# A filter's transform with tables of its own, taken about time 0, and its rows loaded 112 at a time

## The chip, the cores and the metric

The kernel runs on one core of a Trainium2 chip. The metric is the device time of one execution in microseconds; a time given for a kernel is the median of several runs. Besides it there is one execution taken by the hardware profiler, with every instruction's start and length on each engine: PE (matrix products), DVE (vector), ACT (activations, with tables loaded in sets), POOL (which here mostly issues loads) and SP (which issues stores).

## The reference, cut to what matters

Two layers stand behind each other. The first is an attention without softmax, `out = q (k^T v)`, divided by the root mean square over a head's 64 columns and multiplied by `g_norm`. Its output is `x`, of shape batch 8, sequence 576, width 512. The second layer is

```
proj = x @ w_proj                       # 512 -> 3 * 512
x1, x2, x3 = the three thirds of proj
X2 = rfft(x2, n=576, axis=1)            # along the sequence
H  = rfft(filter_fft, n=576, axis=0)    # of the weights: the same for every batch
x2_conv = irfft(X2 * H, n=576, axis=1)
out = (x1 * x2_conv * x3) @ w_out
```

The change is about `H`: it needs the input `filter_fft` (576 rows of 512 numbers) alone, and is computed once, while batch 0 is on its way.

## The kernel before, in words

Everything is held with at most 128 rows. The sequence of 576 is split by a factor of three: three thirds of 192 (SB), each of them folded about its middle, so that a real transform becomes products with cosines and with sines of half length. Frequencies come in groups g = 0, 1, 2: the multiples of 3 (97 of them, N1), and the others in a group of 128 and one of 64. Times are taken in the middle between samples (the odd numbers of `tvi`), so that time reversal maps the grid onto itself.

The tables are made at the start. `tvi` (L120) holds odd numbers, `kcol` (L155) the frequencies; for three columns c, DVE reduces the angle to one turn (L169 to L172, tile `ang`), and ACT takes the absolute value and two sines (L173, L175, L176) into `IV`, which has 288 columns (TH). `IV` serves the inverse transform, of which it uses 192 columns. For the forward transform `tables()` (L187) turns it around with PE transposes into PSUM tiles `ps_ft`, and DVE copies these into `FW` and `FX` (L205 to L210). Column blocks a = 0, 1, 2 of 128, 128 and 32 times are made; blocks beyond 192 serve the filter only.

The filter: `fa` holds rows of `filter_fft` in the order of the grid and `fc` the rows of reversed time, gathered by an indirect DMA with the row numbers `fidx` (L136 to L148). `fold_filter()` (L315) adds and subtracts them into `ff`. `gen_h(g)` (L332) multiplies `ff` with `FW` into a PSUM tile `ps_h`. As the grid stands half a sample beside time 0, the result has to be turned by a phase: `ph` (L163, L164) holds its cosine and sine, `cf` and `pc` the same times the scale of the inverse transform; ACT takes one product (L355, tile `hu`) and DVE the other with the sum (L356), which gives `HH` and `HM`; ACT makes a negative copy (L358).

What sets the order. Each engine has one queue, and its order is fixed when the program is built, by a scheduler that starts from the program's text and keeps some instructions where they stand (`keep_in_program_order`). PSUM has four slots of two banks (`ps_tile`, and `psp.tile` in `tables`); a tile waits for the reader of the one that had its slot. In batch 0 the text goes: `warm` (products that keep PE busy), `qtr(0)`, `warm`, then for both halves `kv`, `att_o`, `att_r`, `att_x`, `fold`; `tables()`; `proj2(0)` (L363: x2, by PE, copied by ACT); `fold_filter()`; `proj13(0, 0)` and `proj13(0, 1)` (L428 and L434); `gen_h(1)`, `gen_h(0)`, `qtr(1)`, `gen_h(2)`, `kv(1)`; and after it the attention of batch 1 mixed with the transforms `fft(0, g)`, whose products with `HH` and `HM` are L408, L409 and L417. From batch 1 on the filter is only read.

POOL issues all loads. In the order of issue: q of batch 0 in two parts, k and v of batch 0 in six, `w_proj` in three, `fa` in three, `fc` in three, q, k and v of batch 1, `w_out`. There are eight semaphores for such loads, so a load waits until the one issued eight before it has landed. The small integer tables (iota) are made on POOL before the first k load.

Of the kernel before, what the change touches and what calls it, by code (L numbers as in the profile page):

```python
# [15 lines left out]
P = 128  # L16
# [4 lines left out]
def kernel(  # L21
# [95 lines left out]
    tvi = work.tile([P, 2 * SB], I32, name="tvi", tag="yg", bufs=3)  # L117


    nc.gpsimd.iota(tvi, pattern=[[2 * SB, 2], [2, 3], [6, 64]], base=1, channel_multiplier=0)  # L120
# [18 lines left out]
    for a, r0, n, base in ((0, 0, 64, 0), (0, 64, 64, 1), (1, 0, 64, 2), (1, 64, 64, SB), (2, 0, 32, SB + 1)):  # L139
        nc.gpsimd.iota(fidx[r0:r0 + n, a:a + 1], pattern=[[0, 1]], base=S - 1 - base, channel_multiplier=-3)  # L140
    for r0, n, a, na, base, step in ((0, 64, 0, 2, 0, 2), (64, 64, 0, 2, 1, SB - 1), (0, 32, 2, 1, SB + 1, 1)):
        nc.gpsimd.dma_start(out=fa[r0:r0 + n, a:a + na], in_=bass.AP(
            tensor=moe_filter_fft.tensor, offset=moe_filter_fft.offset + base * DM,
            ap=[[3 * DM, n], [step * DM, na], [1, DM]]))
    for a in range(3):
        n = P if a < 2 else 32
        nc.gpsimd.indirect_dma_start(out=fc[:n, a], out_offset=None, in_=moe_filter_fft,
                                     in_offset=bass.IndirectOffsetOnAxis(ap=fidx[:n, a:a + 1], axis=0))  # L148
# [7 lines left out]
    tv = work.tile([P, TH], FP32, name="tv", tag="yg", bufs=3)  # L156
    nc.vector.tensor_copy(out=tv, in_=tvi[:, 0:TH])
    IV = consts.tile([P, 6, TH], BF16)
    asc = consts.tile([P, 3], FP32)
    cf = consts.tile([P, 3, 3], FP32)  # L160
    ph = consts.tile([P, 2, 3], FP32)

    nc.scalar.activation(out=ph[:, 0], in_=kcol, func=AF.Sin, scale=-W0, bias=cosb[:, 0:1])  # L163
    nc.scalar.activation(out=ph[:, 1], in_=kcol, func=AF.Sin, scale=W0)  # L164
    for c, tag in enumerate(("x", "Y", "g13")):

        ang = work.tile([P, 2, TH], FP32, name="ang", tag=tag, bufs=1 if c else 2)
# [9 lines left out]
    tc.keep_in_program_order(nc.scalar.preload_act_table_set("abs_reciprocal_sqrt_and_small"))  # L177
# [6 lines left out]
    FW = consts.tile([P, 3, 6, P], BF16)  # L184
    FX = consts.tile([P, 4, P], BF16)

    def tables():  # L187
        nc.vector.memset(FX[0:96, 0], 0.0)
        fts = [psp.tile([P, 2, 8, P], BF16, name="ps_ft", tag="ps") for _ in range(2)]
        lo, hi = slice(0, 64), slice(64, P)  # L190
        tr = nc.tensor.transpose
        for a in range(3):
            n = P if a < 2 else 32
            ts = slice(a * P, a * P + n)
            d = fts[a // 2][:n, a % 2]
            for i in range(6):
                tr(d[:, i], IV[:, i, ts], ident)
            if a == 0:
                tr(d[96:P, 6], IV[:, 1, 0:32], ident)
                for i in (lo, hi):  # L200
                    tr(d[i, 7], IV[:, 1, 32:96], ident)
            if a == 1:
                for i in (3, 5):
                    tr(d[hi, 6 + i // 5], IV[:, i, P:SB], ident)
            nc.vector.tensor_copy(out=FW[:n, a], in_=d[:, 0:6])  # L205
            if a == 0:
                nc.vector.tensor_copy(out=FX[96:P, 0], in_=d[96:P, 6])
                nc.vector.tensor_copy(out=FX[:, 1], in_=d[:, 7])
            if a == 1:
                nc.vector.tensor_copy(out=FX[hi, 2:4], in_=d[hi, 6:8])  # L210
# [104 lines left out]
    def fold_filter():  # L315
        ff = hst['ff'] = work.tile([P, 2, 3, DM], BF16, name="ff", tag="ff")
        for i, op in enumerate((nc.vector.tensor_add, nc.vector.tensor_sub)):
            for r, c in ((slice(0, P), slice(0, 2)), (slice(0, 32), slice(2, 3))):
                tc.keep_in_program_order(op(out=ff[r, i, c], in0=fa[r, c], in1=fc[r, c]))

        nc.vector.memset(asc, 2.0 / S)
        nc.vector.memset(asc[0:1, 0:1], 1.0 / S)
        nc.vector.memset(asc[96:97, 0:1], 1.0 / S)
        for i in range(2):
            nc.vector.tensor_mul(out=cf[:, i], in0=ph[:, i], in1=asc)
        nc.vector.tensor_scalar_mul(out=cf[:, 2], in0=cf[:, 1], scalar1=-1.0)
        pc = hst['pc'] = consts.tile([P, 4], FP32, name="pc")
        for r, o in ((slice(0, 64), (0, 1, 2, 0)), (slice(64, P), (2, 0, 0, 1))):
            for i in range(4):
                nc.gpsimd.tensor_copy(out=pc[r, i:i + 1], in_=cf[r, o[i], 2:3])  # L330

    def gen_h(g):  # L332

# [3 lines left out]
        for ri in range(2):  # L337
            for a in range(3):
                m = P if a < 2 else 32
                kw = dict(start=(a == 0), stop=(a == 2))  # L340
                if g < 2:
                    nc.tensor.matmul(hp[:n, ri], FW[:m, a, 2 * g + ri, 0:n], ff[:m, ri, a], **kw)
                else:
                    for dup in range(2):
                        nc.tensor.matmul(hp[dup * NM:(dup + 1) * NM, ri], FW[:m, a, 4 + ri, ri * NM:(ri + 1) * NM], ff[:m, ri, a], **kw)
# [298 lines left out]
```

## Time and profile before

| | |
|---|---|
| median of 9 runs | 241.28 us (239.31 to 243.04) |
| the profiled execution | 241.06 us |
| its span | 239.0 us |
| busy: PE, DVE, ACT, POOL | 216.4, 197.1, 156.3, 74.1 us |
| TensorE clock granted, mean | 0.976 |
| moved by loads and stores | 27.17 MB |

The stages, from the busy time of each engine in five stretches of the span (us; the last columns are the share of time in which the DMA engines were busy, which can pass 1 since packets overlap, and GB/s):

| stretch | what runs | PE | DVE | ACT | POOL | DMA | GB/s |
|---|---|---|---|---|---|---|---|
| 0 to 21 | tables, attention of batch 0 | 15.6 | 14.8 | 12.2 | 15.6 | 1.15 | 151 |
| 21 to 33.5 | x2 of batch 0, first projections | 10.1 | 9.0 | 3.7 | 9.2 | 1.36 | 221 |
| 33.5 to 43.3 | the filter, q and kv of batch 1 | 7.3 | 4.5 | 6.8 | 5.2 | 1.48 | 196 |
| 43.3 to 59.4 | transforms of batch 0, attention of batch 1 | 13.5 | 15.1 | 9.9 | 8.1 | 1.38 | 161 |
| 59.4 to 239 | batches 1 to 7 | 170.0 | 153.7 | 123.7 | 36.0 | 0.54 | 93 |

A row of the timeline gives the start and the length in microseconds, the engine, the line of the kernel, the operation, the tile written and the tiles read, how many instructions are merged in the row, and in brackets how long the engine stood idle before it and what it waited for. A row of the chain of waits gives start and length of a step in the chain that ended last; "issue" is time in which the engine waited for nothing that the profile shows. A row of the waits gives who waited for whom, the total, how often, and the longest. In the table of stretches an engine's busy time is followed by the number of its instructions, then come the granted clock, the DMA share and GB/s.

### The profile page before, as it was taken

What the parts mean: (1) busy time and instruction counts of PE and PEld (TensorE: products, weight loads), DVE (VectorE), ACT (ScalarE), POOL (GpSimd) and SP (SyncE); (2) the same over time, 40 slices, a digit from 0 to 9 for tenths busy, and PEclk for the clock granted to TensorE, in tenths of its full rate; (3) what the DMA queues carried; (4) which work ended last, traced back from release to release, by engine and by line L of the source; (5) the groups of instructions that cost most, each with busy time, mean ns of one, the idle gap of its engine ahead of it and who ended that gap; (6) DMA issues with size and microseconds to landing.
All of it is one profiled execution on the core that took longest, in us unless ns stands there. A gap on an engine that the chain in (4) does not pass through costs nothing.

```text
span 239.0 us, 4900 instructions
## 1 busy us (share of the span) xinstructions
PE 216.4 (91%) x1960; PEld 129.5 (54%) x1960; DVE 197.1 (82%) x376; ACT 156.3 (65%) x237; POOL 74.1 (31%) x96
## 2 busy tenths in 40 slices
PE   4978788796999999999999999999999999999960
PEld 1434354364566756665667566656675666566420
DVE  6759474699989798979797989797979897999860
ACT  2754528881797779786977697769776977642520
POOL 7963892491190019000910091001200120021010
PEclk9999999797999999999999999999999999999996
DMA  6999999999099139915993399350033003400345
GB/s 65 161 197 237 215 192 197 191 182 109 3 143 189 55 88 141 196 51 134 109 182 96 91 110 175 103 134 0 4 88 88 3 0 91 132 0 3 95 122 178
DMA packets 45559, 27.17 MB, mean 114 GB/s; under 512 B 22274, under 2 KB 40706, under 8 KB 45538
## 3 DMA queue, kind: packets, MB, share of 16 engines
q0 software_dynamic: 40256, 17.70, 58.7%
q1 hardware_dynamic: 5122, 8.92, 13.9%
q8 instruction: 15, 0.25, 0.4%
q10 hardware_dynamic: 160, 0.26, 0.4%
q14 instruction: 6, 0.05, 0.1%
HBM read 33.69 MB, written 9.44 MB: 180 GB/s over the span
## 4 chain that ended last, share of the span: by engine, by line
PE 63%; ACT 16%; DMA 8%; DVE 5%; POOL 3%; issue 2%; POOLq 0%; DVEq 0%
PE ps_x L428 20%; PE ps_out L488 10%; ACT qT L256 6%; PE ps_x L378 5%; DMA fc<-in_moe_filter_fft_dram,fidx 5%; DMA km<-in_k_dram 3%; PE ps_o L265 3%; PE ps_x L369 3%; PE ps_x L384 2%; ACT kvblk L234 2%; PE ps_r L280 2%; ACT osb L271 2%; PE ps_invo L454 2%; PE ps_inve L454 2%; PE ps_x L372 2%
## 5 line engine op out<-in xcount | busy, mean ns | idle before, releaser
L428 PE MATMUL ps_x<-x,wp 128*128 128x288 bf16 x512 | 68.0, 286 | 2.0 <-DVE FX L210 2.0
L428 PEld LDWEIGHTS <-wp 128*128 128x128 bf16 x512 | 49.8, 98 | 15.8 <-issue 3.1
L411 POOL TENSOR_TENSOR Y<-tpw 128x1024 bf16<-128x1024 f32 (+1 forms) x9 | 21.2, 2357 | 68.9 <-PE ps_x L428 43.2
L434 DVE TENSOR_TENSOR g<-ps_x,x 128x576 bf16<-128x576 f32 x32 | 24.2, 755 | 9.9 <-ACT x L432 9.8
L70 POOL DMA_DIRECT2D km<-in_k_dram x9 | 7.8, 871 | 64.7 <-PE ps_kv L223 64.2
L432 ACT CAST x<-ps_x 128x576 bf16<-128x576 f32 x32 | 20.7, 647 | 10.9 <-PE ps_x L428 10.9
L488 PE MATMUL ps_out<-wo,yg 128*128 128x512 bf16 x112 | 26.6, 379 | 0.0
L281 ACT ACTIVATE rstd<-ps_r,bias_eps 128x576 bf16<-128x576 f32 x32 | 23.3, 742 | 4.8 <-PE ps_r L280 4.7
L496 ACT COPY ot<-ps_out 128x1024 f32<-128x1024 f32 (+1 forms) x17 | 15.9, 937 | 13.8 <-PE ps_out L488 13.8
L266 ACT ACTIVATE sq<-ps_o 128x576 bf16<-128x576 f32 x32 | 20.7, 653 | 6.0 <-PE ps_o L265 5.9
L408 DVE TENSOR_TENSOR tpw<-ps_X,HH 128x1024 f32<-128x1024 f32 (+1 forms) x16 | 19.6, 1223 | 5.3 <-PE ps_X L406 4.4
L271 ACT ACTIVATE osb<-ps_o,g_col 128x576 bf16<-128x576 f32 x28 | 20.8, 742 | 0.0
L409 DVE TENSOR_TENSOR tpw<-ps_X,HH 128x1024 f32<-128x1024 f32 (+1 forms) x16 | 19.4, 1215 | 0.0
L458 ACT COPY os<-ps_invo 128x576 f32<-128x576 f32 x14 | 9.0, 641 | 12.7 <-PE ps_x L372 5.1
L265 PE MATMUL ps_o<-qT,kvblk 128*128 128x288 bf16 x64 | 13.2, 293 | 3.7 <-ACT kvblk L234 2.0
L488 PEld LDWEIGHTS <-yg 128*128 128x128 bf16 x112 | 10.8, 98 | 10.4
L378 PE MATMUL ps_x<-wp,ab 128*128 128x512 bf16 x64 | 15.5, 381 | 0.5 <-DVE ab L307 0.4
L256 ACT COPY qT<-ps_qT 128x1152 bf16<-128x1152 bf16 x14 | 15.1, 1122 | 0.1
L535 PE MATMUL ps_w<-kvblk,ind 128*128 128x512 bf16 x33 | 11.0, 484 | 3.7 <-DVE ind L103 3.4
L79 POOL DMA_DIRECT2D qb<-in_q_dram x16 | 12.6, 788 | 5.0 <-DMA wp<-in_moe_w_proj_dram 3.0
L280 PE MATMUL ps_r<-sq,ind 128*128 128x288 bf16 x64 | 13.3, 290 | 0.9 <-ACT osb L271 0.5
L374 ACT CAST x<-ps_x 128x1024 bf16<-128x1024 f32 x8 | 8.1, 1016 | 9.0 <-PE ps_x L372 9.0
(177 smaller groups left out, 421.0 us busy)
## 6 DMA issues: line engine op xcount, KB each, us to landing
out_dram<-ot SPq DMA_DIRECT2D x28, 256.0 KB, 3.2
qb<-in_q_dram POOLq DMA_DIRECT2D x16, 288.0 KB, 7.3
km<-in_k_dram POOLq DMA_DIRECT2D x7, 512.0 KB, 6.2
vm<-in_v_dram POOLq DMA_DIRECT2D x7, 512.0 KB, 8.6
wp<-in_moe_w_proj_dram POOLq DMA_DIRECT2D x3, 512.0 KB, 11.4
out_dram<-ot SPq DMA_DIRECT2D x10, 128.0 KB, 2.9
km<-in_k_dram POOLq DMA_DIRECT2D x2, 256.0 KB, 5.9
kt<-in_k_dram POOLq DMA_DIRECT2D x8, 64.0 KB, 5.7
```

The costliest lines, as they stand in the source:

```text
L256: nc.scalar.copy(out=o_, in_=i_)
L265: nc.tensor.matmul(op[:, h, 0:TH], kvblk[b % 2][:, j], s['qT'][:, 2 * (j % 2) + j // 2, h * TH:(h + 1) * TH], start=True, stop=True)
L266: nc.scalar.activation(out=s['sq'][:, j].rearrange("p (a b) -> p a b", a=2), in_=op[:, :, 0:TH], func=AF.Square)
L271: nc.scalar.activation(out=o_, in_=op[:, :, 0:TH], func=AF.Copy, scale=g_col)
L281: nc.scalar.activation(out=s['rstd'][:, j].rearrange("p (a b) -> p a b", a=2), in_=r2[:, :, 0:TH], func=AF.Abs_reciprocal_sqrt, scale=1.0 ...
L378: nc.tensor.matmul(pp[:, h], ab[:, j, h * SB:h * SB + P], wp[:, j, DM:2 * DM], start=(j == 0), stop=(j == NDC - 1))
L408: nc.vector.tensor_mul(out=t_[:n, 0], in0=xp[:n], in1=HH[:n, g, 1:3])
L411: nc.gpsimd.tensor_add(out=Y[:n, 2 * g:2 * g + 2], in0=t_[:n, :, 0], in1=t_[:n, :, 1])
L428: nc.tensor.matmul(pp[:, h, 0:TH], w_, x[:, j, h * TH:(h + 1) * TH], start=(j == 0), stop=(j == NDC - 1))
L432: nc.scalar.copy(out=x1, in_=pp[:, :, 0:TH])
L434: nc.vector.tensor_mul(out=st[b]['g13'][:, dc].rearrange("p (a b) -> p a b", a=2), in0=pp[:, :, 0:TH], in1=x1)
L488: nc.tensor.matmul(pp[:, cc], yg[:, dc, c * P:(c + 1) * P], wo[:, dc], start=(dc == 0), stop=(dc == NDC - 1))
```

## The change

The filter's rows are taken about time 0: row n is folded with row 576 - n instead of 575 - n. The phase falls away, and with it `ph`, `cf`, `pc`, `hu` and the pairs of ACT and DVE operations that applied it. Its transform gets tables of its own, `FH`, for 97 times by three and all 289 frequencies: DVE makes the angles in `filter_angles()`, called behind `qtr(0)`, and ACT the sines in `filter_tables()`, called in front of `tables()`. ACT's set of functions has been changed by then, so `filter_tables()` loads the set for sines again, and after it the other one. Since rows 0 and 288 are their own partners, two rows of the cosines are halved.

`IV` has 192 columns now and `FW` two column blocks instead of three. `fa` is loaded in one DMA, 112 rows of three sequence rows each (1536 numbers), `fc` in three gathers of 112 rows; 97 of the 112 are used. In the last part of batch 0 `gen_h(2)` goes in front of `qtr(1)`.

```diff
-    tvi = work.tile([P, 2 * SB], I32, name="tvi", tag="yg", bufs=3)
-    nc.gpsimd.iota(tvi, pattern=[[2 * SB, 2], [2, 3], [6, 64]], base=1, channel_multiplier=0)
+    tvi = work.tile([P, SB], I32, name="tvi", tag="yg", bufs=3)
+    nc.gpsimd.iota(tvi, pattern=[[2, 3], [6, 64]], base=1, channel_multiplier=0)
+    NF = N1 + SB
+    kri = work.tile([P, NF], I32, name="kri", tag="yg", bufs=3)
+    nc.gpsimd.iota(kri[:, 0:N1], pattern=[[3, N1]], base=0, channel_multiplier=0)
+    nc.gpsimd.iota(kri[:, N1:NF], pattern=[[1, 2], [3, SB // 2]], base=1, channel_multiplier=0)
+    tci = consts.tile([P, 3], I32)
+    nc.gpsimd.iota(tci, pattern=[[1, 3]], base=0, channel_multiplier=3)
...
-    for a, r0, n, base in ((0, 0, 64, 0), (0, 64, 64, 1), (1, 0, 64, 2), (1, 64, 64, SB), (2, 0, 32, SB + 1)):
-        nc.gpsimd.iota(fidx[r0:r0 + n, a:a + 1], pattern=[[0, 1]], base=S - 1 - base, channel_multiplier=-3)
-    for r0, n, a, na, base, step in ((0, 64, 0, 2, 0, 2), (64, 64, 0, 2, 1, SB - 1), (0, 32, 2, 1, SB + 1, 1)):
-        nc.gpsimd.dma_start(out=fa[r0:r0 + n, a:a + na], in_=bass.AP(
-            tensor=moe_filter_fft.tensor, offset=moe_filter_fft.offset + base * DM,
-            ap=[[3 * DM, n], [step * DM, na], [1, DM]]))
+    nc.gpsimd.iota(fidx, pattern=[[-1, 3]], base=S, channel_multiplier=-3)
+    nc.gpsimd.memset(fidx[0:1, 0:1], 0)
+    NL = 112
+    nc.gpsimd.dma_start(out=fa[:NL], in_=bass.AP(
+        tensor=moe_filter_fft.tensor, offset=moe_filter_fft.offset, ap=[[3 * DM, NL], [1, 3 * DM]]))
     for a in range(3):
-        n = P if a < 2 else 32
-        nc.gpsimd.indirect_dma_start(out=fc[:n, a], out_offset=None, in_=moe_filter_fft,
-                                     in_offset=bass.IndirectOffsetOnAxis(ap=fidx[:n, a:a + 1], axis=0))
+        nc.gpsimd.indirect_dma_start(out=fc[:NL, a], out_offset=None, in_=moe_filter_fft,
+                                     in_offset=bass.IndirectOffsetOnAxis(ap=fidx[:NL, a:a + 1], axis=0))
...
-    IV = consts.tile([P, 6, TH], BF16)
+    IV = consts.tile([P, 6, SB], BF16)
...
-        ang = work.tile([P, 2, TH], FP32, name="ang", tag=tag, bufs=1 if c else 2)
+        ang = work.tile([P, 2, SB], FP32, name="ang", tag=tag, bufs=1 if c else 2)
...
+    def filter_angles():
+        nc.vector.tensor_copy(out=kr, in_=kri)
+        nc.vector.tensor_copy(out=tcol, in_=tci)
+        a_, r_ = (work.tile([P, 3, NF], FP32, name="fang", tag="ot", bufs=3)[:N1] for _ in range(2))
+        for a in range(3):
+            nc.vector.tensor_scalar_mul(out=a_[:, a], in0=kr[:N1], scalar1=tcol[:N1, a:a + 1])
+        nc.vector.tensor_scalar(out=r_, in0=a_, scalar1=1.0 / S, scalar2=MAGIC, op0=ALU.mult, op1=ALU.add)
+        nc.vector.tensor_scalar(out=r_, in0=r_, scalar1=MAGIC, scalar2=-1.0 * S, op0=ALU.subtract, op1=ALU.mult)
+        nc.vector.tensor_tensor(out=r_, in0=r_, in1=a_, op=ALU.add)
+        fang['ar'] = a_, r_
+
+    def filter_tables():
+        a_, r_ = fang['ar']
+        tc.keep_in_program_order(nc.scalar.preload_act_table_set("trig_and_small"))
+        keep = tc.keep_in_program_order
+        keep(nc.scalar.activation(out=a_, in_=r_, func=AF.Abs))
+        keep(nc.scalar.activation(out=FH[:N1, :, 1], in_=r_, func=AF.Sin, scale=2 * W0))
+        keep(nc.scalar.activation(out=FH[:N1, :, 0], in_=a_, func=AF.Sin, scale=-2 * W0, bias=cosb[:N1, 0:1]))
+        rsqrt_set()
+        for p in (0, 96):
+            nc.vector.tensor_scalar_mul(out=FH[p:p + 1, 0, 0], in0=FH[p:p + 1, 0, 0], scalar1=0.5)
...
     def tables():
...
+        for i in range(2, 6):
+            tr(d0[:, i], IV[:, i, 0:P], ident)
+        tr(d0[0:96, 0], IV[:, 0, 0:96], ident)
+        tr(d0[96:P, 6], IV[:, 1, 0:32], ident)
+        for r in (lo, hi):
+            tr(d0[r, 7], IV[:, 1, 32:96], ident)
+        for i in range(2, 6):
+            tr(d1[lo, i], IV[:, i, P:SB], ident)
+        for i in (3, 5):
+            tr(d1[hi, 6 + i // 5], IV[:, i, P:SB], ident)
+        cp(out=FW[:, 0, 2:6], in_=d0[:, 2:6])
+        cp(out=FW[lo, 1, 2:6], in_=d1[lo, 2:6])
+        cp(out=FX[hi, 2:4], in_=d1[hi, 6:8])
+        cp(out=FW[0:96, 0, 0], in_=d0[0:96, 0])
+        cp(out=FX[96:P, 0], in_=d0[96:P, 6])
+        cp(out=FX[:, 1], in_=d0[:, 7])
...
     def fold_filter():
         ff = hst['ff'] = work.tile([P, 2, 3, DM], BF16, name="ff", tag="ff")
         for i, op in enumerate((nc.vector.tensor_add, nc.vector.tensor_sub)):
-            for r, c in ((slice(0, P), slice(0, 2)), (slice(0, 32), slice(2, 3))):
-                tc.keep_in_program_order(op(out=ff[r, i, c], in0=fa[r, c], in1=fc[r, c]))
...
+            tc.keep_in_program_order(op(out=ff[:N1, i], in0=fa[:N1], in1=fc[:N1]))
...
     def gen_h(g):
...
-                    nc.tensor.matmul(hp[:n, ri], FW[:m, a, 2 * g + ri, 0:n], ff[:m, ri, a], **kw)
+                    nc.tensor.matmul(hp[:n, i], FH[:m, a, 1 - i, f0:f0 + n], ff[:m, 1 - i, a], **kw)
...
-            nc.scalar.activation(out=u[:n, i], in_=hp[:n, ri], func=AF.Copy, scale=c1)
-            nc.vector.scalar_tensor_tensor(out=o_, in0=hp[:n, 1 - ri], scalar=c2, in1=u[:n, i], op0=ALU.mult, op1=ALU.add)
-        if g < 2:
-            nc.scalar.activation(out=HH[:n, g, 2], in_=HH[:n, g, 0], func=AF.Copy, scale=-1.0)
+        if g == 2:
+            nc.scalar.activation(out=HM, in_=hp, func=AF.Copy, scale=2.0 / S)
+            return
+        nc.scalar.activation(out=HH[:n, g, 0:2], in_=hp[:n], func=AF.Copy, scale=asc[:n] if g == 0 else 2.0 / S)
+        nc.vector.tensor_scalar_mul(out=HH[:n, g, 2], in0=HH[:n, g, 0], scalar1=-1.0)
...
     qtr(0)
+    filter_angles()
     warm(9)
...
+    filter_tables()
     tables()
...
             gen_h(0)
+            gen_h(2)
             qtr(1)
-            gen_h(2)
             kv(1)
```

## The prediction

> **What bounds the kernel now.** The profiled execution took 241.06 us, its span 239.0: 2.06 us lie around the span and are left alone. The rows of 40 slices show PE at nine tenths from slice 10 on, so everything after about 60 us is PE's and identical in both programs (the built order on each engine differs only in the names of DMA semaphores there). What the change touches ends before 45 us, so I read that stretch of the chain of waits:
>
> ```profile
> 7.84 7.20 DMA km<-in_k_dram
> ...
> 17.28 11.08 DMA fc<-in_moe_filter_fft_dram,fidx
> ...
> 28.48 0.13 DVE ff L319
> 28.61 1.02 issue
> 29.62 0.55 DVE FW L205
> 30.17 0.01 issue
> 30.19 0.30 DVE FX L210
> 30.49 0.04 issue
> 30.53 3.10 PE ps_x L428 x24
> 33.63 3.43 PE ps_h L342 x12
> ...
> 43.25 0.53 PE ps_o L265 x2
> ```
>
> The reader is to see one thread: the gathered filter rows fc land at 28.36; only then DVE can run ff; queued behind that first ff on DVE stand the copies of FW and FX, which hold a PSUM slot that L428 needs. PE stands still from 28.53 to 30.53. The groups of waits confirm both ends:
>
> ```profile
> DVE ff L319 <- DMA fc<-in_moe_filter_fft_dram,fidx: 3.3, 1, 3.3
> ...
> PE ps_x L428 <- DVE FX L210: 2.0, 1, 2.0
> ```
>
> From 43.25 (the first ps_o of batch 1) DVE runs almost without a gap until batch 1's projection starts at 59.40; its first product, at 45.22, waits for ps_X behind ps_o. So **the change is worth what it moves ps_o at 43.25.**
>
> **The change, part by part.**
>
> *Startup.* IV, ang and tv shrink from 288 to 192 columns. With a tensor-tensor at 448 ns for 288 and 1226 for 1024, DVE costs 0.144 us plus 1.057 ns a column; the angle operations lose about 1 us, and casts and two of the three new L196 products take it up again (0.31 + 0.17 + 0.8). Worth nothing either way: PE warms up until 9.4 and qT is copied at 10.15. POOL's iotas gain 0.5 us net (0.51 for 384 columns, 0.12 for one, so 0.31 + 0.22 + 0.31 + 0.12 and gaps against 0.51), before the first k load. The last first-half load (vt, issued at 7.16, 5.0 us to land) is there at 12.16, wanted at 12.74: hidden by 0.08; without that cover at most 0.5.
>
> *filter_angles on DVE.* In the built order an L197 and an L198 (97x867) stand before and between the two copies of kvblk at 13.14, an L199 behind. No row has 867 columns. L170 takes 295 ns for 288: 0.89 if all of it scales, 0.6 if 0.144 is fixed; the row's fixed part is the better founded, I take 0.6. L197 fits before 13.14, L198 delays the second copy and with it ps_o and all of batch 0's attention by **0.6** (0.3 at the least, 1.0 at the most). L199 (0.144 + 867 x 1.057 = 1.06) hides while ACT squares.
>
> *tables().* 14 transposes before the first projection instead of 15, none in the middle of it instead of 8 (saves PE 0.6). But two FW copies now stand ahead of the second x and d_ on DVE, and the first waits for PE's transposes, which end near 22.05. Copy 0.4, x 0.7, copy 0.4: d_ starts at 23.55 instead of 22.25. Everything behind it (ab, rr) is **1.3** later, the 0.6 included. From PE's rows: L378 at 24.7, rr's L369 at 25.6, then L372 0.6, L378 0.5, L384 1.0, four groups of L428 of 1.03: PE reaches the filter at **32.3** (before: 33.47). FX and FW wait for the cosine instead of fc, and are done near 27.0; the stall of 2.0 is gone.
>
> *filter_tables on ACT.* Two table loads, Abs and two Sin of 867 columns come between the last rstd (20.65, now 21.25) and the first copy of x2. ACT at 0.43 for 288 and 0.65 for 576 gives 0.2 + 0.78 ns a column; starts 0.1 apart inside: 0.78 + 0.78 + 0.97 (0.09 more for a bias column, as L281 against L266).
>
> ```profile
> 10.32 0.61 ACT L176 ACTIVATE IV<-ang,cosb 128x288 bf16<-128x288 f32 x1
> 10.95 1.28 ACT L177 ACT_TABLE_LOAD   x1
> 14.24 1.19 ACT L266 ACTIVATE sq<-ps_o 128x576 bf16<-128x576 f32 x2 [2.01 <-PE ps_o L265]
> ```
>
> The row: a load costs 1.28 and starts 0.02 after the activation in front of it. So 1.28 + 2.53 + 1.28 = 5.09, done at 26.34; x2 is ready at 26.7. It fits in ACT's idle 5.31 us. The rule that speaks against this edit is in the Trainium skill, "ScalarE: Activation LUTs", What ACT_TABLE_LOAD costs: a switch of sets is 1.28 us plus a drain of 1.38, about 2.66, so functions should be batched by set. The trace shows no drain ahead of the load, and none can be seen behind it, since ACT then idles until 14.24. By the rule ACT ends at 29.1, x2's three copies at 31.7 instead of 28.8, three groups of L428 wait a little each, and PE is at the filter by 33.2: 0.4 past the landing path below. I take the row; the rule costs 0.4 of the gain.
>
> *The loads.* fa and fc grow from 576 KB each to 672 (112 rows of 6 KB; three gathers of 112 rows), in fewer DMAs. POOL lets a load go when the one eight before it has landed; there are two fewer, so the gathers go out near 13 to 17 instead of 15.9 to 20. That gains nothing by itself: wp's last part lands at 24.15 (10.85 + 13.3), and fa and fc behind it in the same queue took 4.4 us for 1152 KB (to 28.55). 1344 KB take 5.1: **29.3**. Bounds: 28.4 if 6 KB rows move faster and the deeper queue fills the DMA share that sinks to 1.0 around 25, 31 if they move at the 196 GB/s of the loads before. The next q, k and v go out earlier, behind them; kv(1) needs v by 38, landed at 37.6 before.
>
> *ff.* Two operations of 97x1536, 1.69 apart, 1.77 the last (0.144 + 1536 x 1.057): done 3.5 after landing, **32.8**. Before, four operations and two copies took until 32.93. So the filter starts at 32.8, by landing, with PE ready 0.5 sooner.
>
> *gen_h and behind it.* Gone: six L355, six L356, POOL's eight pc copies (3.26 us, hidden). New: three ACT copies of 1024 columns and two small DVE products, hidden. gen_h(2) goes ahead of qtr(1), so on ACT the copy HM stands ahead of qT. From the start of the filter: 3.43 (L342) + 1.75 (L345's 1.84 less its overlap) + 1.05 for HM (L374: 1.02) + 2.1 (qT twice) + 0.75 (kvblk) + 0.05 = 9.15; before it was 43.25 - 33.47 = 9.78. With L378's 0.237 us a matmul in place of L342's 0.286 it is 8.5. ps_o at 42.0 or 41.3; the middle, **1.6 us earlier**.
>
> **Sum.** 241.06 - 1.6 = 239.5. The median of the runs shown, 241.28, lies 0.2 above this execution: forecast 239.7. Ends: startup 0.3 to 1.0 and table drains touch only PE's side, which has 0.5 to spare; landing 28.4 to 31 moves the sum by +0.5 (then PE binds) to -1.7.
>
> **Rivals.**
>
> 1. *The gain is larger because PE's clock holds.* After the idle stretch before 43.25 PE runs at half speed:
>
> ```profile
> 42.00:43.00 1.00, 0.00 (x0) 0.00 (x0) 0.31 (x1) 0.99 (x4) 0.85 (x1) 1.00 1.50 196
> 43.00:44.00 1.00, 0.75 (x3) 0.37 (x4) 0.45 (x1) 0.66 (x2) 1.00 (x3) 0.71 1.63 185
> 44.00:45.00 1.00, 1.00 (x4) 0.11 (x2) 0.67 (x1) 1.00 (x3) 0.59 (x1) 0.50 1.71 186
> 45.00:46.00 1.00, 1.00 (x6) 0.62 (x5) 0.86 (x2) 0.59 (x2) 0.00 (x0) 0.50 1.65 189
> ```
>
> (The third number from the end is the granted clock.) With no hole between gen_h and qtr the drop may not come: ps_o to ps_X then takes about 1.2 instead of 1.9, total gain 2.4: 238.9. Against: 1.7 us of idle before ps_o remain.
>
> 2. *The gain is eaten up by the same clock at another place.* PE now waits for ab from about 23.0 to 24.7. A drop there for 3 us (as long as the one above) costs 1.5 us: PE at the filter by 33.8, gain 0.6: 240.7. For: two such gaps (42.0 and 54.3) were followed by half clock. Against: the gap of 2.0 at 28.53 was not.
>
> 3. *Slower: the landing.* One mechanism: the 112-row transfers move no faster than the loads in front. 1344 KB at 196 GB/s from 24.15 plus the 0.5 us that POOL starts late is 31.5, and with an engine trailing by another 0.5, 32.0. Every microsecond past 28.8 counts in full; ps_o is late from 30.9 on. 32.0 gives 35.5 for ff, 44.6 for ps_o, 1.35 late: 242.6. For: the profile has no 6 KB row, and DMA never rests up to there. Against: the 2 KB rows of the same tensor moved at 238 to 291 GB/s between 21 and 26.
>
> **How the numbers follow.** Forecast (gain 0.9 to 2.2) 0.50, rival 1 0.13, rival 2 0.22, rival 3 0.10, something unlisted 0.05. What a measurement can tell from no change is 0.5%, 1.2 us. Faster by more: most of the forecast and rival 1, 0.58; within: the rest of it and rival 2, 0.30; slower: 0.12. The range 238.4 to 241.6 leaves out rival 3 and the ends of rival 1.
>
> **What would show it.** PE without a stall of 2 us on FX; kvblk's second copy about 0.6 us late; ACT's block of two loads some 5.1 us long and no wait of PE on x2; DVE ff waiting for fc until about 29.3; gen_h starting within 0.1 of ff's end; batch 1's first ps_o near 41.7; an equal distance from there to the end. Wrong, if L428's matmuls or x2's copies end after ff, or fc lands outside 28.4 to 31.

## The result, and the profile after

The changed kernel takes 238.53 us (median of 17 runs, 237.44 to 242.01); the kernel before, run beside it, 240.81 (54 runs). The ratio is 0.9899, with an interval of 0.9874 to 0.9924: 2.4 us (1.8 to 3.0) or 1.0% faster. The forecast was 239.7, a gain of 1.6 us on the 241.28 known then: the direction was right and the median lies just inside the lower end of the range (238.4), but the size was too small. The profiled execution took 238.56 us, its span 236.6 (before: 239.0), mean clock 0.977.

The same stretch of the chain of waits, now of the changed kernel (start, length, what):

```profile
16.46 13.34 DMA fc<-in_moe_filter_fft_dram,fidx
...
29.92 1.26 DVE ff L350
31.18 0.41 issue
31.60 1.76 DVE ff L350
33.36 0.04 issue
33.41 2.78 PE ps_h L364 x12
36.19 1.44 PE ps_h L368 x12
37.63 0.02 issue
37.65 1.02 ACT HM L370
38.68 2.03 ACT qT L288 x2
40.71 0.25 ACT kvblk L266
...
41.39 0.65 PE ps_o L297 x2
```

The chain runs through the very steps of the forecast: fc's landing, ff, the filter's matmuls, HM, qT, kvblk, ps_o. But look at the starts. The kernel before had, on PE's timeline:

```profile
33.47 3.58 PE L342 MATMUL ps_h<-ff,FW 128*128 128x512 bf16 x12
```

The filter begins at 33.41, where it began at 33.47: nearly nothing was gained up to there. From there to ps_o it takes 7.98 us instead of 9.78. So ps_o is 1.86 us earlier, but with other parts than forecast: the forecast had 0.67 at the filter's start, where 0.06 came, and 0.95 behind it, where 1.80 came. The waits of the changed kernel for 22 to 46 us:

```profile
DVE ff L350 <- DMA fc<-in_moe_filter_fft_dram,fidx: 2.2, 1, 2.2
...
PE ps_o L297 <- ACT kvblk L266: 2.0, 1, 2.0
```

The stall on FX is gone. PE still stands for 2.0 us ahead of ps_o, for ScalarE. Behind ps_o the distance is kept: VectorE's d_ starts 1.76 earlier (49.56), its u 1.78 (57.48), kv of batch 2 2.00 (61.68). In the one profiled execution of before, PE ran at half clock from 57 to 60.8, and not in that of after; the step from 1.78 to 2.00 goes with it. From there to PE's last matmul it is 168.2 us in both traces, as in those of all runs here (168.17 to 168.23): what happens behind kv of batch 2 is only shifted. The remaining 0.4 of the span lies behind PE's end, at the last stores: 7.10 us before, 6.73 after, and 6.68 to 7.06 in the other runs. So the last 0.6 of the 2.4 us differ from execution to execution, and the runs do not show that they are the change's.

Why was the filter not sooner? At the start, filter_angles() delays kvblk's second copy, as said: batch 0's first ps_o comes at 14.28 instead of 13.79 (0.49; 0.6 was predicted). Then this happens (PE's timeline and stretches of the changed kernel; in the stretches the third number from the end is the granted clock):

```profile
14.28 1.14 PE L297 MATMUL ps_o<-qT,kvblk 128*128 128x288 bf16 x4 [1.22 <-DVE kvblk L264]
...
28.99 4.09 PE L443 MATMUL ps_x<-x,wp 128*128 128x288 bf16 x32
...
14.00:15.00 1.00, 0.72 (x4) 0.46 (x5) 0.97 (x2) 0.03 (x1) 0.70 (x2) 0.57 1.34 183
15.00:16.00 1.00, 1.00 (x4) 0.43 (x3) 0.66 (x2) 1.00 (x2) 1.00 (x1) 0.50 1.24 201
16.00:17.00 1.00, 1.00 (x5) 0.58 (x4) 1.00 (x2) 0.38 (x2) 0.69 (x2) 0.50 1.23 205
17.00:18.00 1.00, 1.00 (x4) 0.30 (x2) 0.20 (x1) 1.00 (x2) 1.00 (x2) 0.72 1.26 208
```

PE has stood for 1.2 us and runs on at half clock, where before it had 1.00 throughout. d_ starts at 24.37 instead of 22.25: 2.1 late, where 1.3 was predicted, and PE is ready for the filter at 33.08 instead of 32.3. Meanwhile fc lands at 29.80 (29.3 predicted), and ff ends at 33.36 (32.8). The two paths end 0.3 us apart.

The half clock is not the program's alone. Nine kernels, the changed one and eight below, have this startup as it is here, and in the profiles of all of them PE stands for 1.22 or 1.23 us ahead of this ps_o. In six of them half clock followed, and L443 was done 18.8 to 18.9 us after ps_o's start. In three the clock stayed at 1.00, and it took 17.8 to 18.0, so that PE was ready at 31.9 to 32.4. One of the three (PE's timeline of the run below that puts the order of ff's halves on top of the loads held back):

```profile
14.29 0.66 PE L299 MATMUL ps_o<-qT,kvblk 128*128 128x288 bf16 x4 [1.22 <-DVE kvblk L266]
...
28.00 4.09 PE L445 MATMUL ps_x<-x,wp 128*128 128x288 bf16 x32
```

The block of two table loads on ScalarE (timeline of the changed kernel):

```profile
22.16 1.28 ACT L204 ACT_TABLE_LOAD   x1
23.45 0.93 ACT L206 ACTIVATE fang<-fang 97x867 f32<-97x867 f32 x1
...
25.10 1.01 ACT L208 ACTIVATE FH<-fang,cosb 97x867 bf16<-97x867 f32 x1
26.13 1.28 ACT L182 ACT_TABLE_LOAD   x1
27.58 1.01 ACT L389 CAST x<-ps_x 128x1024 bf16<-128x1024 f32 x1 [0.16 <-PE ps_x L387]
```

5.25 us from the first load to the end of the second; 5.09 were predicted by the row, 7.85 by an estimate from the Trainium skill's rule of a drain at each switch ("ScalarE: Activation LUTs", What ACT_TABLE_LOAD costs). No drain is seen ahead of a load (0.02 us), and none behind: the next operation starts 0.01 us after the first load, and the copy behind the second waits 0.16 for PE. The row was right to take.

### The profile page after: what moved, and what is told of

Its sections match the earlier page's. It is cut to its first block, busy times and chain, and to the rows that moved or that the text cites. A ratio compares the mean times of both kernels' runs of the same rounds, so it can differ in the third digit from the quotient of the medians.

```text
span 236.6 us, 4864 instructions
## 1 busy us (share of the span) xinstructions
PE 213.6 (90%) x1951; PEld 129.3 (55%) x1951; DVE 195.7 (83%) x377; ACT 158.9 (67%) x235; POOL 70.6 (30%) x86
## 3 DMA queue, kind: packets, MB, share of 16 engines
q1 hardware_dynamic: 5122, 8.92, 14.3%
## 4 chain that ended last, share of the span: by engine, by line
PE 62%; ACT 15%; DVE 7%; POOL 6%; DMA 6%; issue 2%; POOLq 0%; DVEq 0%
PE ps_x L443 19%; PE ps_out L503 10%; ACT qT L288 6%; DMA fc<-in_moe_filter_fft_dram,fidx 6%; PE ps_x L393 6%; PE ps_o L297 3%; PE ps_x L399 2%; PE ps_x L384 2%; ACT kvblk L266 2%; PE ps_r L312 2%; ACT osb L303 2%; PE ps_invo L469 2%; PE ps_inve L469 2%; ACT sq L298 2%; PE ps_kv L255 2%
## 5 line engine op out<-in xcount | busy, mean ns | idle before, releaser
L443 PE MATMUL ps_x<-x,wp 128*128 128x288 bf16 x512 | 67.8, 286 | 0.0
L443 PEld LDWEIGHTS <-wp 128*128 128x128 bf16 x512 | 49.8, 98 | 13.6 <-issue 0.9
L297 PE MATMUL ps_o<-qT,kvblk 128*128 128x288 bf16 x64 | 13.8, 305 | 4.8 <-ACT kvblk L266 2.7
L321 DVE TENSOR_TENSOR x<-osb,rstd 128x1152 bf16<-128x1152 bf16 x16 | 12.3, 767 | 1.0 <-ACT rstd L313 1.0
```

The lines of the kernel that those rows point to most:

```text
L297: nc.tensor.matmul(op[:, h, 0:TH], kvblk[b % 2][:, j], s['qT'][:, 2 * (j % 2) + j // 2, h * TH:(h + 1) * TH], start=True, stop=True)
L443: nc.tensor.matmul(pp[:, h, 0:TH], w_, x[:, j, h * TH:(h + 1) * TH], start=(j == 0), stop=(j == NDC - 1))
```

## The experiments

Theory A: the filter starts when ff and PE are both there, and from its start to ps_o ScalarE's copies and PE's matmuls make the chain. The rivals differ from run to run and stand in the expectations. All ratios are against the kernel before, run beside each.

**The order of work.** In the changed kernel:

```diff
             gen_h(0)
-            gen_h(2)
             qtr(1)
+            gen_h(2)
```

> The changed kernel with gen_h(2) put behind qtr(1) again. Theory A (behind the filter's start ScalarE's copies are a chain, and the change took copies out of it; their order matters little): the same five copies of ScalarE stand in another order and the 0.31 us in which ScalarE waited for ps_h of L368 goes; batch 1's first ps_o stays at 41.0 to 41.4 us, ratio to the kernel before 0.988 to 0.990. Theory B (the new order is a good part of the gain): ps_o 0.7 us or more later than in the changed kernel, ratio 0.992 or more.

The filter started at 33.59 and ps_o came at 41.14, as A had it: 7.55 us instead of 7.98, so the new order costs 0.4 here. But the ratio was 0.9961 (0.9941 to 0.9981), 1.5 us worse than the changed kernel. Something behind ps_o took back more than was gained; it is found below. Its rows:

```profile
33.59 2.78 PE L364 MATMUL ps_h<-ff,FH 97*128 97x512 bf16 x12
...
41.14 0.42 PE L297 MATMUL ps_o<-qT,kvblk 128*128 128x288 bf16 x2 [1.55 <-ACT kvblk L266]
...
46.89 4.35 DVE L321 TENSOR_TENSOR x<-osb,rstd 128x1152 bf16<-128x1152 bf16 x1
```

The same move alone in the kernel before:

```diff
             gen_h(0)
-            qtr(1)
             gen_h(2)
+            qtr(1)
```

> The kernel before with nothing but the new order, gen_h(2) ahead of qtr(1). Theory A (ScalarE's conversions are the chain): L345 still waits about 1.1 us or more for the PSUM tile that VectorE's L356 lets go, and qT now stands behind two more L355 of 0.7; ps_o 1 to 2 us later than 43.25, ratio 1.004 to 1.008. Theory B (the order is a good part of the gain): ps_o 0.7 us or more earlier, ratio 0.997 or less.

Measured: 1.0076 (1.0047 to 1.0104), 1.8 us slower. ps_o came at 45.76, later than theory A had it: 1.26 of the 2.51 us are the new order's (11.04 from the filter's start instead of 9.78), and the filter started 1.25 late because in this execution PE ran at half clock from 30.4 to 33.5. The order is no part of the gain.

**The stall on FX, alone.** In the kernel before, `keep_in_program_order` around the copies of FW and FX:

> The kernel before with the copies of FW and FX held in program order, so that they stand ahead of ff on VectorE: the stall of 2.0 us at L428 alone is taken away. Theory A: PE is ready for the filter near 31.6, ff ends near 31.9, gen_h starts near 31.9 instead of 33.47, everything behind it is as far away as before; ratio 0.993 to 0.995 (1.2 to 1.6 us). Theory B (the stall's gain is taken back behind it, by the loads of k and v or by ScalarE): ratio 0.998 to 1.000.

Measured: 0.9939 (0.9918 to 0.9959), 1.5 us. Its trace (PE's timeline):

```profile
31.02 3.70 PE L343 MATMUL ps_h<-ff,FW 128*128 128x512 bf16 x12
36.94 1.84 PE L346 MATMUL ps_h<-ff,FW 128*64 128x512 bf16 x12 [1.09 <-DVE HH L357]
40.91 0.42 PE L266 MATMUL ps_o<-qT,kvblk 128*128 128x288 bf16 x2 [1.38 <-ACT kvblk L235]
```

The filter starts at 31.02, even sooner than the 31.9 expected, since the first products need only the first half of ff; ps_o is 2.34 earlier than in before. So the stall was worth all that was hoped from it. (In the two profiled executions the distance is kept: kv of batch 2 comes 2.33 earlier. That the ratio gives 1.5 is a matter of executions: the profiled one of before lies 0.6 above its median here, this one 0.4 below.) The changed kernel removes it too, and pays it back: its PE is ready only at 33.08, its larger load of fc lands 1.4 us later than before (29.80 against 28.36), and its gen_h takes first the half of ff that is made last (`1 - i` in L364), so that no product can start on the first half made.

**The startup.** In the changed kernel `filter_angles()` moved behind the first half of batch 0:

```diff
     qtr(0)
-    filter_angles()
     warm(9)
...
         fold(0, jj)
+        if jj == 0:
+            filter_angles()
```

> The changed kernel with filter_angles() behind the first half of batch 0, so that its L198 does not stand between the copies of kvblk. Theory A (the filter's start is held by fc's landing at 29.8 plus 3.5, with PE ready only 0.3 sooner): the half clock from 14 to 17.5 goes, PE is ready 0.5 to 1.5 sooner, and gen_h still starts at 33.3 to 33.5; ratio 0.988 to 0.992, as the changed kernel. Theory F (the startup's delay is paid in full at the end): ratio 0.985 or less.

The clock stayed at 1.00 from 14 to 18, and PE was ready at 32.0, 1.1 sooner. It waited for ff:

```profile
34.29 1.91 PE L364 MATMUL ps_h<-ff,FH 97*128 97x512 bf16 x8 [2.29 <-DVE ff L350]
```

In this execution fc landed near 30.7, so the filter began later still, at 34.29, outside the expected stretch, and ps_o came at 42.27. The ratio was 0.9900 (0.9858 to 0.9942), the changed kernel's. The startup's delay is hidden behind the landing. (Though its ps_o is 0.88 later, VectorE's first product behind it, tpw, starts at 43.49, as in the changed kernel's profile, 43.48, where PE ran at half clock between the two.) With the loads of fa and fc moved ahead as well (`load_wp` is the loop that is taken out, for the thirds named):

```diff
-    for part in (1, 0, 2):
-        load_w(wp[:, :, part * DM:(part + 1) * DM], ...)
+    load_wp(1)
     (loads of fa and fc)
+    load_wp(0, 2)
```

> The changed kernel with its two startup prices taken away: filter_angles() stands behind the first half of batch 0, so that it does not come between the two copies of kvblk, and fa and fc are loaded ahead of the first and last third of w_proj. Theory A (the filter starts when both ff and PE are there; fc's landing at 29.8 and PE at 33.1 each hold it near 33.4): kvblk's second copy by 13.95, no half clock from 14 to 17.5, fc lands by 26, gen_h starts at 31.5 to 32.2 and the first ps_o stands at 39.5 to 40.2 instead of 41.39. The total then depends on whether GpSimd's additions meet VectorE's x: without it 0.983 to 0.985, with it up to 0.996. Theory B (PE is late for w_proj instead): gen_h at 33.0 or later.

ff now started at 27.32 and waited for no landing. But then w_proj's last third was late:

```profile
PEld L447 <- DMA wp<-in_moe_w_proj_dram: 1.0, 1, 1.0
```

gen_h began at 33.2 to 33.4 and ps_o stood at 41.18: theory B. All these loads are issued by GpSimd into one queue, and here what was moved forward pushed another wait into its place. The ratio was 0.9935 (0.9901 to 0.9969), with x of L325 (L321 elsewhere) stretched to 4.48 us.

**The order of ff's halves.** In the changed kernel:

```diff
-        for i, op in enumerate((nc.vector.tensor_add, nc.vector.tensor_sub)):
+        for i, op in ((1, nc.vector.tensor_sub), (0, nc.vector.tensor_add)):
```

> The changed kernel with the difference of ff made ahead of the sum, since its gen_h takes the difference first. Theory A (ff and PE both hold the start): the first six products of gen_h need only the first operation, done 1.8 after fc's landing, so the start is PE's, 33.0 to 33.5, whatever the landing; where PE is ready before ff's second half the second six still wait for it. Gain 0.1 us where ff and PE end together as in the profile of the changed kernel, 0.5 to 1.0 in executions whose fc lands after 30.3: ratio 0.986 to 0.990. Rival: an earlier ps_o meets the lock-out of VectorE's x and the ratio is 0.993 or more.

VectorE's ff started at 30.33, late, and the filter all the same at 32.96:

```profile
32.96 2.98 PE L364 MATMUL ps_h<-ff,FH 97*128 97x512 bf16 x12
...
41.15 0.42 PE L297 MATMUL ps_o<-qT,kvblk 128*128 128x288 bf16 x2 [1.34 <-ACT kvblk L266]
```

The start is PE's now, and the order of the halves was why the landing bound it. The ratio, 0.9887 (0.9828 to 0.9946), is not told apart from the changed kernel's. The rival's mechanism was there in this profile, x of L321 lasting 4.07 us; what it cost the interval doesn't tell.

**The pace of the matmuls.** In the changed kernel's gen_h, leaving out the third chunk's rows from 32 on:

```diff
-                m = N1 if a == 0 else N1 - 1
+                m = (N1, N1 - 1, 32)[a]
```

> The changed kernel with 32 rows instead of 96 in the third chunk of gen_h's sums; rows 32 on of that chunk are left out of the filter. It asks why a matmul of gen_h took 0.286 us before (rows 128, 128, 32) and 0.232 after (97, 96, 96). If a chunk of 32 rows breaks the pace: L364 x12 back at 3.3 to 3.5 us. If the pace came from the tables' layout or the transfers: 2.7 to 2.9 us.

```profile
34.10 3.60 PE ps_h L364 x12
37.70 1.79 PE ps_h L368 x12
...
43.26 0.42 PE ps_o L297 x2
```

With fewer rows to multiply, the twelve matmuls take 3.60 us instead of 2.78, at a granted clock of 1.00 in both. A chunk of 32 rows between chunks of 96 breaks the pace (0.300 us each instead of 0.232). And the whole stage, 34.10 to 43.26, is 9.16 us, where the forecast had 9.15. That the two agree to 0.01 is chance: the two groups of matmuls took 0.2 more than the forecast's terms, what follows them 0.2 less. It is one execution.

**ScalarE's conversion.** In the kernel before, plain copies out of ps_h, leaving out the turn by the phase (shown in extracts):

```diff
-            nc.scalar.activation(out=u[:n, i], in_=hp[:n, ri], func=AF.Copy, scale=c1)
-            nc.vector.scalar_tensor_tensor(out=o_, in0=hp[:n, 1 - ri], scalar=c2, in1=u[:n, i], ...)
...
-            nc.scalar.activation(out=HH[:n, g, 2], in_=HH[:n, g, 0], func=AF.Copy, scale=-1.0)
...
+        nc.scalar.activation(out=HH[:n, g, 0:2], in_=hp[:n], func=AF.Copy, ...)
+        nc.vector.tensor_scalar_mul(out=HH[:n, g, 2], in0=HH[:n, g, 0], scalar1=-1.0)
```

> The kernel before with plain copies out of ps_h in place of the phase: three copies on ScalarE as in the changed kernel, and the negative on VectorE, instead of six L355, six L356 and two L358; tables, loads, order and rows are those of before. The turn by the phase is left out of the filter. Theory A (ScalarE's conversion is what stands between the filter's start and ps_o): the start stays at 33.5, ps_o comes at 41.7 to 42.0 instead of 43.25, all behind it as much earlier; ratio 0.993 to 0.996. Theory E (what counted was the pace of the matmuls and the tables): ps_o at 43.0 or later, ratio 0.998 or more.

```profile
33.73 3.58 PE L342 MATMUL ps_h<-ff,FW 128*128 128x512 bf16 x11
...
42.08 0.42 PE L265 MATMUL ps_o<-qT,kvblk 128*128 128x288 bf16 x2 [1.25 <-ACT kvblk L234]
```

From the filter's start to ps_o it took 8.35 us instead of 9.78: the conversion is worth 1.4 there. Yet the ratio was 0.9993 (0.9952 to 1.0033), neither theory's at the end. The profiled execution was the shortest of its twelve (239.59 against a median of 241.29), and even in it d_ took 3.15 us.

**What takes a gain at ps_o back.** In the changed kernel the copies of qT of batch 1 went to VectorE (`if b == 0` became `if b < 2` in qtr):

> The changed kernel with the two copies of qT of batch 1 on VectorE instead of ScalarE. Theory A (ScalarE's chain HM, qT, kvblk sets ps_o): kvblk starts when kv(1) ends near 39.3, ps_o at 39.9 to 40.1 instead of 41.39, and all behind it as much earlier; ratio 0.983 to 0.985. Theory B (PE, or the landing of k and v, would end as late anyway, or the half clock takes it back): ps_o later than 40.8, ratio 0.988 or more.

ps_o came at 39.96, as A had it. And the ratio was 0.9961 (0.9942 to 0.9980), worse than the changed kernel. VectorE's and GpSimd's timelines in this run:

```profile
45.71 5.31 DVE L321 TENSOR_TENSOR x<-osb,rstd 128x1152 bf16<-128x1152 bf16 x1
...
45.03 2.36 POOL L426 TENSOR_TENSOR Y<-tpw 128x1024 bf16<-128x1024 f32 x1
...
48.05 2.35 POOL L426 TENSOR_TENSOR Y<-tpw 97x1024 bf16<-97x1024 f32 x1
```

and in the changed kernel itself:

```profile
48.02 0.95 DVE L321 TENSOR_TENSOR x<-osb,rstd 128x1152 bf16<-128x1152 bf16 x1
48.89 0.74 DVE L449 TENSOR_TENSOR g<-ps_x,x 128x576 bf16<-128x576 f32 x1
49.56 2.25 DVE L331 TENSOR_TENSOR d__656<-x 128x768 bf16<-128x768 bf16 x1
...
45.99 2.37 POOL L426 TENSOR_TENSOR Y<-tpw 128x1024 bf16<-128x1024 f32 x1 [1.02 <-ACT rstd L313]
...
49.02 2.36 POOL L426 TENSOR_TENSOR Y<-tpw 97x1024 bf16<-97x1024 f32 x1
```

and d_ in the kernel before:

```profile
51.32 2.26 DVE L299 TENSOR_TENSOR d__675<-x 128x768 bf16<-128x768 bf16 x1
```

The same x, 0.75 us when it runs alone, takes 5.31: it ends 0.6 us after GpSimd's second addition. d_ is held by that addition in the changed kernel, as in before (2.26 us instead of 0.54). g, one of whose inputs is in PSUM, runs its 0.74 beside it unhindered. The Trainium skill, "SBUF — State Buffer", Who interferes with whom, states it: a VectorE operation with two inputs in SBUF contends with a GpSimd operation that reads SBUF, and the pair of ports that they share is an exclusive lock. The traces agree (0.75 us alone, 5.31 beside the additions), and add one thing: x was also held over the 0.7 us between the two additions, which GpSimd spends on a load's issue. In this run the first addition is late, at 45.03, because GpSimd issues a load of v of batch 3 from 44.13 until then. Holding these loads back on top of that edit (`keep_in_program_order` on them):

> The kernel with qT of batch 1 on VectorE, and the loads of k and v of batch 3 held behind GpSimd's two additions Y of batch 0. Theory C (a VectorE operation with two SBUF inputs stands still while GpSimd adds; in the run without this edit x of L321 lasted 5.31 us because the first addition began only at 45.03, behind a load's issue): the additions now run from about 43.55 to 48.2, x ends by 48.9 instead of 51.02 and d_ by 50.1 instead of 52.15; ratio 0.980 to 0.984. Theory D (L321 was late for another reason, such as the cores' memory traffic): x still lasts over 4 us, ratio 0.994 or more.

```profile
46.56 0.95 DVE L323 TENSOR_TENSOR x<-osb,rstd 128x1152 bf16<-128x1152 bf16 x1
...
48.11 2.03 DVE L333 TENSOR_TENSOR d__656<-x 128x768 bf16<-128x768 bf16 x1
```

x ends at 47.5 and d_ at 50.1, although this execution's ps_o came only at 40.82. The ratio is 0.9797 (0.9744 to 0.9850): 4.9 us faster than before, and the interval lies below the changed kernel's. The other way, again with qT on VectorE, the additions on VectorE:

```diff
-                nc.gpsimd.tensor_add(out=Y[...], ...)
+                (nc.gpsimd if b else nc.vector).tensor_add(out=Y[...], ...)
```

> The kernel with qT of batch 1 on VectorE, and the two additions Y of batch 0 on VectorE too, 2.3 us more for it; GpSimd computes nothing there. Theory C (lock-out by GpSimd's additions): x of L321 lasts 0.75 and d_ of L331 0.54, d_ ends near 49.8 in spite of the 2.3 us, ratio 0.980 to 0.984. Theory D: x or d_ is stretched as before, ratio above 0.994.

Measured: 0.9819 (0.9764 to 0.9874), with x at 0.75 and d_ at 0.55 us. Theory C twice. (When d_ ends can't be compared: the profiled execution, the longest of the seven, ran the filter at half clock, 4.08 us for L364, and its ps_o came at 43.72.) All edits that helped, together:

> All edits that helped in one: qT of batch 1 on VectorE, the loads of batch 3 behind GpSimd's additions, filter_angles() behind the first half, and fa and fc ahead of the last third of w_proj alone. Expected: fc lands by 28, gen_h starts at 32.2 to 33.0, ps_o at 39.3 to 40.2, x and d_ of batch 1 end no later than in the run without the last two edits; ratio 0.976 to 0.980. If the landing of v of batch 1 (38.6 in the changed kernel) is the wall: ps_o not before 39.9 and the ratio within 0.2% of the run without them.

gen_h began at 32.88 and ps_o stood at 40.60, 0.4 later than expected; its chain leads through vt of batch 1, which landed at 39.02. The ratio was 0.9820 (0.9762 to 0.9879), not told apart from the run with the loads held back alone. The next wall is the landing of batch 1's loads. The last run puts the order of ff's halves on top of the loads held back:

> The same edit on top of the kernel with qT on VectorE and batch 3's loads behind the additions, where the filter started at 34.12, 1.0 after PE was ready. Theory A: the start at 33.0 to 33.6, ps_o at 40.0 to 40.4 instead of 40.82, bounded by the landing of v of batch 1; ratio 0.976 to 0.980. Rival (that landing is the wall already): within 0.1% of 0.980.

The filter's first three products ran at 32.19, the other nine at 33.86 behind ff's second half; ps_o stood at 40.55, just outside what was expected, and its chain leads through v again (vt landed at 38.97). The ratio of 0.9770 (0.9716 to 0.9825) is the lowest of all, and not told apart from the 0.9797 without this edit: it is lower because the kernel before was slower beside it (242.43 against 240.89); the medians of the two are 236.67 and 236.57.

**The parts, without the lock-out.** Four kernels run side by side, each with batch 0's additions on VectorE: before, before with plain copies, the changed kernel, before with its copies ahead of ff.

> The kernel before with GpSimd's two additions Y of batch 0 on VectorE; nothing else. In the profile of before the lock-out costs 1.9 us (0.23 at x, 1.7 at d_), two additions of 1.14 on VectorE cost 2.3, so by the profile alone it is 0.3 to 0.5 us slower, ratio 1.001 to 1.002. Theory C (executions of before differ in how long x is held, which the one profile doesn't show): the slow end of its executions goes, ratio 0.991 to 0.997. Theory D (they differ by the clock alone): ratio 1.000 or more, the spread as wide as before.

> The kernel before with plain copies out of ps_h (the turn by the phase is left out of the filter) and with the two additions on VectorE. Theory A with C (taking out ScalarE's conversion is worth 1.2 to 1.4 us, which the additions had swallowed): 1.2 to 1.4 us faster than the kernel before with the additions on VectorE, its ps_o near 42.0. Theory E (it is worth nothing at the end): within 0.4 us of it.

> The changed kernel with the two additions of batch 0 on VectorE. By its profile the lock-out costs it 1.9 us and the additions 2.3, with g of L449 moved behind fold: within 0.4 us of the changed kernel, ratio 0.988 to 0.992, x 0.75 us, d_ 0.54. Against the kernel before with the same edit it shows what the change is worth without the lock-out: 1.9 to 2.0 us by ps_o. If the gain of the change was partly a matter of the lock-out: less than 1.2 us.

> The kernel before with the copies of FW and FX ahead of ff and the two additions on VectorE. Theory A (the stall at L428 alone held all behind it): 2.0 to 2.4 us faster than the kernel before with the additions on VectorE, as ps_o was 2.34 sooner. If less than 1.6: the stall's gain is lost behind ps_o for another reason than the additions.

| kernel, additions on VectorE | ratio to before | against the first row |
|---|---|---|
| before | 1.0016 (0.9999 to 1.0033) | |
| before, plain copies | 0.9962 (0.9932 to 0.9992) | 1.3 us (0.5 to 2.1) |
| changed | 0.9908 (0.9891 to 0.9925) | 2.6 us (2.0 to 3.2) |
| before, copies ahead of ff | 0.9947 (0.9926 to 0.9967) | 1.7 us (1.0 to 2.3) |

(The second row leaves out the turn by the phase. The last column is the difference of the two ratios times 240.45 us; half its interval is the root of the two halves' squares.) In the changed kernel with this edit x and d_ run at their own length:

```profile
48.76 0.75 DVE L321 TENSOR_TENSOR x<-osb,rstd 128x1152 bf16<-128x1152 bf16 x1
...
50.56 0.55 DVE L331 TENSOR_TENSOR d__656<-x 128x768 bf16<-128x768 bf16 x1
```

The conversion's 1.3 us now reach the end, where with the lock-out 0.2 had come of them (from 1.1 lost to 1.2 gained); the two intervals still overlap. The whole change is worth as much without the lock-out as with it, so the lock-out is no part of its gain: by their profiles both kernels lose the same 1.9 us to it. That the executions of before differ by it (theory C on the first of the four) is not borne out; its ratio is what the profile gave. For the stall 1.7 us were measured, less than the 2.0 to 2.4 expected by its 2.34 at ps_o, though the interval reaches 2.3; whether anything is lost between is not settled. The profiled execution of that last kernel was the longest of its seven and stood still for 1.9 us near 17 for nothing that its core's trace shows, so it is not read.

## Why the prediction was right, and where it was wrong

**Right:** what bounds the start (fc's landing, then ff), the vanished stall, kvblk's delay (0.49 for 0.6), the table block (5.25 for 5.09), the chain behind the filter step by step, and that the gain at ps_o goes through to the end.

**The step that failed** is the size of "gen_h and behind it": 9.15 us, or 8.5 at a faster pace, of which the sum took the middle, 8.8. Measured are 7.98. Its chain was the right one (its terms add up to 9.13, not 9.15). The terms that were too large are 3.43 for L342's twelve matmuls and 1.75 for L345's, taken from rows whose third chunk has 32 rows. The changed chunks have 97, 96 and 96. They took 2.78 and 1.44: 0.96 us less, and qT, kvblk and HM another 0.2. The run with 32 rows put back takes 3.60 and 1.79 again, and 9.16 in all. The faster pace had been named as a bound by another row (0.237 a matmul), for L342 alone; 0.232 was the pace, and for L345 too it was faster. Why a chunk of few rows slows the matmuls is open.

Measured by parts, each in one execution, the stage's 1.80 us are: 1.43 for the conversion (9.78 to 8.35 in the plain copies), 0.65 for L364 against L342, 0.15 that no run separates, and 0.43 back for the new order. The prediction lists the conversion's operations as gone and gives them no price of their own; they are in its sum, since the sum is made over the new chain, but a reader would not look for the largest part there.

**The start of the filter** was 0.6 too early: 32.8 predicted, 33.41 measured. The landing was 0.5 later, within its bounds (VectorE's ff started at 29.6 to 30.8 in the changed kernel and the variants that kept the order of its loads), and it held all of gen_h only because of the order of ff's halves, which the prediction didn't look at. PE came 0.8 later because of half clock from 14 to 17.5; in the three executions without it PE was ready at 31.9 to 32.4, as predicted. Rival 2 had this clock drop, at another place: the wait of 1.3 us ahead of 25.5 kept clock 1.00. The two errors, 0.6 too much at the start and 0.85 too little behind it, partly cancelled at ps_o by luck (1.6 predicted, 1.86 measured). Of the 0.8 us by which the gain passed the forecast, these are 0.26. The rest came behind ps_o in the two profiled executions, 0.2 with the clock near 57 to 61 and 0.4 at the last stores, and its cause stays open.

**Rival 1**, the clock behind ps_o, did not come true in the profiled execution: 0.50 from 42 to 44. That its number, 2.4 us, was measured is chance as far as this execution shows. In ten of the eleven variants of the changed kernel tpw starts 1.21 to 1.23 us behind ps_o instead of 2.09, in the one with its additions on VectorE at a clock of 1.00; but so it does in the kernel before with plain copies (1.22), so the runs don't show that a held clock is the change's. **Rival 3** did not happen.

## What to carry to other kernels

A stall that is removed is worth what the next path allows: here the stall alone gave 1.5 us, and the change that removed it spent nearly all of that on a later landing and a later PE before its other parts earned 1.8 at ps_o. Take a matmul's duration from a row with the same mix of rows, not from the operation that it replaces. And before a gain is carried to the end of a kernel, lay VectorE's two-input operations beside GpSimd's computing: three edits that made ps_o 0.2 to 1.4 us earlier than in the changed kernel ended 0.9 to 1.5 us behind it (by the ratios). In all three x was held for 4.35 to 5.31 us and d_ ended at 52.2 to 52.5 instead of 51.8; that the lock-out is the cause was tested for one of them, qT on VectorE, where taking it away gave 0.9797 and 0.9819.

## What the runs showed that was not expected

- x of L321 is let in when the first addition has 0.34 to 0.37 us left (changed kernel, before, stall removed: 0.95 to 0.98 us long), and held until the second has ended when 0.43 or more is left (halves of ff exchanged 0.43: 4.07; order back 0.71: 4.35; loads ahead 0.83: 4.48; qT on VectorE 1.68: 5.31). Less than a tenth of a microsecond can decide over three. Why it isn't let in between the additions is open.
- Half clock follows some idle stretches of PE and not others: in the changed kernel 1.2 us ahead of 14.3 brought it and 1.3 ahead of 25.5 did not. The same stretch at the same place does both: 1.22 us ahead of batch 0's ps_o were followed by it in six executions and not in three; 2.0 ahead of batch 1's ps_o were in the changed kernel, and 1.9 with the additions on VectorE were not. The length of the stretch does not decide it alone, and what does is open.
- In the chain the first ff is cut to 1.26 us and 0.41 of "issue" follow. VectorE did not stand there: by its own records the first ff lasts 1.75 us, and the second starts 0.07 before it ends. The second gather's issue on GpSimd took 1.74 us, the others 1.03 and 0.92.
